# The last chunk of a Fourier-mixing and MLP kernel: sums on VectorE, products read in PSUM, output from three queues

## Chip, cores and metric

One Trainium2 chip, one NeuronCore. The metric is the device time of one execution in microseconds (us). The kernel before takes about 2004 us. Runs with a profile also give the span, from the first to the last recorded instruction, which is 1.8 us less than the time. Two runs of the same kernel can differ by 4 us and more, so this document also uses a measure inside one profile, the **tail**: from the start of the last matmul to the end of the span.

## The reference

```python
def _attn_ref(x):                        # x: 8 x 3008 x 256, float32
    X = np.fft.fft(x, axis=1)
    X = np.fft.fft(X, axis=2)
    return X.real.astype(np.float32)

def _moe_ref(x, w_in, w_out):            # x: 24064 x 256, d_ff 2048
    h = x @ w_in
    relu6 = np.clip(h + 3.0, 0.0, 6.0)
    g = h * relu6 / 6.0
    return (g @ w_out).astype(np.float32)
```

The output of the first goes, reshaped to 24064 x 256, into the second.

## The kernel before

The kernel works through four pairs of batch rows, twelve chunks a pair, eight steps (`fc`) a chunk. In each step TensorE makes the hidden layer (`mlp1`), VectorE and ScalarE gate it, GpSimd forms four sums of the gated blocks (`combine`), and TensorE adds seven products into four PSUM banks (`mlp2`, a seven-multiplication scheme for a 2 x 2 block product). After the last step of a chunk, ScalarE evicts the four banks, GpSimd forms the four output blocks (`finish`), VectorE transposes them in 32 x 32 blocks and SyncE sends them out (`store`). For every chunk but the last of all, `finish` and `store` run beside the next chunk's matmuls. For the last of all, nothing is left to run beside.

```python
    def combine(ch, fc):
        ...
        add(cn[:, 0:2], a[:, 2:3].to_broadcast([P, 2, ch.n]), a[:, 3::-3])
        add(cn[:, 2], cn[:, 0], a[:, 0])
        add(cn[:, 3], a[:, 1], cn[:, 2])
        ch.c[fc] = cn

    def add(out, in0, in1):
        nc.gpsimd.tensor_tensor(out, in0, in1, op=AL.add)

    def mlp2(ch, fc):
        ...
        for i, mv in enumerate(moving):
            ...
            nc.tensor.matmul(ch.acc[i // 2][:, i % 2, 0:ch.n], G[:, i, fc, :], mv, ...)
            if fc == NF - 1 and (i % 2 == 1 or i == 6):
                ...
                k = 2 * (i // 2)
                nc.scalar.mul(ch.e[:, k:i + 1, 0:ch.n], ch.acc[i // 2][:, 0:i + 1 - k, 0:ch.n], 1.0 / WS)

    def finish(ch):
        ...
        add(rn[:, 0, 0], e[:, 0], e[:, 1])
        nc.gpsimd.tensor_tensor(wn[:, 0], e[:, 0], e[:, 5], op=AL.subtract)
        add(wn[:, 1:3], wn[:, 0:1].to_broadcast([P, 2, n]), e[:, 4:2:-1])
        add(rn[:, 0, 1], wn[:, 2], e[:, 6])
        add(rn[:, 1], wn[:, 1:2].to_broadcast([P, 2, n]), e[:, 2:4])

    def store(ch, m):
        ...                              # two transposes, then:
            for qd in range(DB):
                nc.sync.dma_start(out=out_k[...], in_=o[...])
    ...
    # behind the loop over all steps:
    finish(prev)
    for m in range(2):
        store(prev, m)
```

GpSimd also issues all loads of `x` and of the weights: 84 transfers (`nc.gpsimd.dma_start` and the indirect form), the last of them some 630 us before the end.

## Time and profile before

| | before |
|---|---|
| median of 3 runs | 2004.42 us (2000.66 to 2004.54) |
| span of the profiled run | 2002.9 us |
| TensorE busy | 98% |
| start of the last matmul | 1989.4 us |
| end of the last transpose | 1993.95 us |
| start of the last output issue | 2000.0 us |
| end of the span | 2002.9 us (tail 13.5 us) |

The table is to be read from the bottom. TensorE is the bound for 1989 us. Behind its last matmul come 13.5 us in which it has nothing to do: 4.5 us of evictions, sums and transposes, then some 9 us in which only transfers and the closing exchange between engines are left. The change is about these 13.5 us, 0.7% of the time. The views that show this are in the prediction.

### The profile page before, as it was taken

To read this page: it belongs to the slowest core of one execution; us is meant where nothing else is said; L and a number is where in the kernel's file an instruction comes from. 1 tells how busy PE (TensorE), PEld (TensorE's weight loads), DVE (VectorE), ACT (ScalarE), POOL (GpSimd) and SP (SyncE) were. 2 spreads that over 40 slices of the span, in tenths; PEclk is the share of its full clock that TensorE was granted. 3 is DMA by queue.
4 is the path that set the end of the run, shared out by engine and by line. 5 is a ranking of instruction groups with operands and counts; after the bars stand their busy time and mean duration, and the time that the engine had idled before them with its cause. 6 is when DMAs were issued, how large, how long until landed. Compare 5 with 4: busy or idle time off the path is not lost.

```text
span 2002.9 us, 28366 instructions
## 1 busy us (share of the span) xinstructions
PE 1965.6 (98%) x9178; PEld 1691.5 (84%) x9178; DVE 1437.2 (72%) x2701; ACT 701.2 (35%) x1198; POOL 1417.9 (71%) x1612
## 2 busy tenths in 40 slices
PE   9899999999999999999999999999999999999997
PEld 5488888888888888888888888888888888888886
DVE  5677767776777777776777767777678777777775
ACT  6533333333333333333333333333333333333332
POOL 3277778776777787777658877778666667667665
PEclk9899999999999999999999999999999999999998
DMA  9512211211112122110201221112110101101100
GB/s 275 162 27 59 51 40 48 55 38 35 28 35 51 41 51 56 50 51 25 48 18 30 69 56 39 51 43 53 35 27 20 27 17 27 32 12 27 27 11 19
DMA packets 158985, 93.54 MB, mean 47 GB/s; under 512 B 131019, under 2 KB 143819, under 8 KB 158838
## 3 DMA queue, kind: packets, MB, share of 16 engines
q1 hardware_dynamic: 149366, 58.22, 12.1%
q0 software_dynamic: 9472, 33.49, 6.1%
q8 instruction: 75, 1.23, 0.3%
q14 instruction: 72, 0.59, 0.1%
HBM read 54.32 MB, written 37.33 MB: 46 GB/s over the span
## 4 chain that ended last, share of the span: by engine, by line
PE 93%; DVE 3%; ACT 1%; issue 0%; POOL 0%; DVEq 0%; POOLq 0%; ACTq 0%
PE acc L379 55%; PE v L325 16%; PE u L325 16%; PE ps L280 2%; PE ps L226 2%; DVE a L357 1%; ACT t L354 0%; DVE u L338 0%; DVE s L330 0%; ACT PM L457 0%; PE wps L522 0%; DVE o L405 0%; DVE v L344 0%; DVE u L341 0%; PE ps L223 0%
## 5 line engine op out<-in xcount | busy, mean ns | idle before, releaser
L369 POOL TENSOR_TENSOR c<-a 128x512 f32<-128x512 f32 (+1 forms) x384 | 478.4, 1246 | 454.9 <-PE acc L379 358.1
L379 PE MATMUL acc<-c,G 128*128 128x256 f32 (+1 forms) x3072 | 712.1, 375 | 0.0
L354 ACT ACTIVATE t<-u,half 128x512 f32<-128x512 f32 (+2 forms) x416 | 272.4, 655 | 1104.6 <-DVE u L338 1092.9
L379 PEld LDWEIGHTS acc<-c,G 128*128 128x128 f32 x3072 | 577.5, 190 | 72.7
L330 DVE SCALAR_TENSOR_TENSOR s<-qn,WN,u 128x256 f32<-128x256 f32 x768 | 334.6, 477 | 351.6 <-PE u L325 351.2
L379 PE MATMUL acc<-a,G 128*128 128x256 f32 (+1 forms) x2304 | 551.2, 375 | 0.0
L379 PEld LDWEIGHTS acc<-a,G 128*128 128x128 f32 x2304 | 434.6, 190 | 57.6
L325 PE MATMUL v<-q,W 127*128 127x256 f32 x1536 | 397.7, 381 | 7.7 <-DVE a L357 7.7
L325 PE MATMUL u<-q,W 128*128 128x256 f32 x1536 | 395.4, 380 | 2.5 <-DVE a L357 2.2
L325 PEld LDWEIGHTS u<-q,W 128*128 128x128 f32 x1536 | 287.8, 190 | 59.9 <-issue 15.8
L325 PEld LDWEIGHTS v<-q,W 127*128 127x128 f32 x1536 | 289.7, 190 | 55.6 <-issue 8.2
L357 DVE SCALAR_TENSOR_TENSOR a<-t,u 128x512 f32<-128x512 f32 (+2 forms) x416 | 266.1, 646 | 95.7 <-ACT t L354 90.3
L369 POOL TENSOR_TENSOR c<-c,a 128x256 f32<-128x256 f32 (+1 forms) x384 | 274.7, 715 | 30.1
L369 POOL TENSOR_TENSOR c<-a,c 128x256 f32<-128x256 f32 (+1 forms) x384 | 274.6, 715 | 30.1
L338 DVE TENSOR_TENSOR u<-s,v 128x512 f32<-128x512 f32 (+1 forms) x384 | 263.1, 685 | 41.5 <-DVE s L330 0.9
L354 ACT ACTIVATE t<-v,half 128x512 f32<-128x512 f32 (+1 forms) x384 | 257.1, 670 | 5.8 <-DVE v L344 4.5
L344 DVE TENSOR_TENSOR v<-v,s 128x512 f32<-128x512 f32 (+1 forms) x384 | 257.9, 672 | 1.1
L357 DVE SCALAR_TENSOR_TENSOR a<-t,v 128x512 f32<-128x512 f32 (+1 forms) x416 | 255.4, 620 | 0.5
L369 POOL TENSOR_TENSOR r<-w,e 128x256 f32<-128x256 f32 (+1 forms) x96 | 92.2, 981 | 3.8
L385 ACT ACTIVATE e<-acc 128x512 f32<-128x512 f32 (+1 forms) x192 | 87.0, 543 | 2.9 <-PE acc L379 2.8
L405 DVE STREAM_TRANSPOSE o<-r 128x256 f32<-128x256 f32 (+1 forms) x192 | 72.5, 416 | 6.6 <-POOL r L369 6.4
L238 ACT COPY z<-ps 96x512 f32<-96x512 f32 x64 | 37.2, 581 | 83.5 <-PE ps L226 63.1
(81 smaller groups left out, 754.0 us busy)
## 6 DMA issues: line engine op xcount, KB each, us to landing
out_dram<-o SPq DMA_DIRECT2D x736, 32.0 KB
zd<-z SPq DMA_DIRECT2D x32, 384.0 KB
g<-zd SPq DMA_DIRECT2D x48, 256.0 KB
xt<-in_x_dram POOLq DMA_DIRECT2D x21, 384.0 KB, 4.0
qn<-qd SPq DMA_DIRECT2D x23, 256.0 KB
st<-in_moe_w_in_dram POOLq DMA_DIRECT2D x8, 512.0 KB, 11.8
st<-in_moe_w_out_dram POOLq DMA_DIRECT2D x8, 512.0 KB, 5.7
xt<-in_x_dram POOLq DMA_DIRECT2D x7, 376.0 KB, 3.9
```

The lines of the kernel that those rows point to most:

```text
L226: nc.tensor.matmul(ps[0:PZ], F[0:PR, 0:PZ], y[:, 2 * i:2 * i + 2, :], start=True, stop=True)
L280: nc.tensor.matmul(ps[:, blk, 2 * u:2 * u + 2], g[:, kk, blk * (P + 1):blk * (P + 1) + P], T[:, :, gr, blk, kk], start=True, stop=True)
L325: nc.tensor.matmul(ps[:, i], W1[r, blk, f * P:(f + 1) * P], q[r, blk, of:of + KC], start=True, stop=True)
L330: nc.vector.scalar_tensor_tensor(s[:, i].rearrange("p k n -> p (k n)"), qn[:, of * N2:(of + KC) * N2], WN[:, f:f + 1], u[:, i].rearrange(" ...
L338: nc.vector.tensor_tensor(u[:, :, 0:ns], s[:, :, 0:ns], v[:, :, 0:ns], op=AL.add)
L344: nc.vector.tensor_tensor(v[:, :, 0:nm], v[:, :, 0:nm], s[:, :, 0:nm], op=AL.subtract)
L354: nc.scalar.activation(t, h, AF.Relu, bias=half[:], scale=scale)
L357: nc.vector.scalar_tensor_tensor(dst, t, 1.0, h, op0=AL.min, op1=AL.mult)
L369: nc.gpsimd.tensor_tensor(out, in0, in1, op=AL.add)
L379: nc.tensor.matmul(ch.acc[i // 2][:, i % 2, 0:ch.n], G[:, i, fc, :], mv, start=(fc == 0 and i % 2 == 0), stop=(fc == NF - 1), skip_group_c ...
L385: nc.scalar.mul(ch.e[:, k:i + 1, 0:ch.n], ch.acc[i // 2][:, 0:i + 1 - k, 0:ch.n], 1.0 / WS)
L405: nc.vector.transpose(o[:, 0:n // DH, h], ch.r[:, m, h, 0:n].rearrange("p (j i) -> p j i", i=DH))
```

## The change

Its intent is to shorten the tail. (1) The last step's `combine` runs on VectorE, which is free by then. (2) The last chunk's sums run on VectorE, and the products 4, 5 and 6 are read directly in PSUM by a fused multiply-add, so two evictions go. (3) The 16 output transfers are dealt out over SyncE, ScalarE and GpSimd in turn.

```diff
+            self.final = self.last and pr.p == NP - 1
...
+        eng = nc.vector if ch.final and fc == NF - 1 else nc.gpsimd
+        add(cn[:, 0:2], a[:, 2:3].to_broadcast([P, 2, ch.n]), a[:, 3::-3], eng)
+        add(cn[:, 2], cn[:, 0], a[:, 0], eng)
+        add(cn[:, 3], a[:, 1], cn[:, 2], eng)
...
+                if ch.final and k >= 4:
+                    continue
                 nc.scalar.mul(ch.e[:, k:i + 1, 0:ch.n], ...)
...
+    def finish_final(ch):
+        ...
+        def add_product(out, i, in1, sign=1.0):
+            nc.vector.scalar_tensor_tensor(out, ch.acc[i // 2][:, i % 2, 0:n], sign / WS, in1,
+                                           op0=AL.mult, op1=AL.add)
+        add(rn[:, 0, 0], e[:, 0], e[:, 1], nc.vector)
+        turn(ch, os[0], 0, 0)
+        add_product(wn[:, 0], 5, e[:, 0], -1.0)
+        add(wn[:, 2], wn[:, 0], e[:, 3], nc.vector)
+        add_product(rn[:, 0, 1], 6, wn[:, 2])
+        turn(ch, os[0], 0, 1)
+        send(ch, os[0], 0)
+        add_product(wn[:, 1], 4, wn[:, 0])
+        for h in range(2):
+            add(rn[:, 1, h], wn[:, 1], e[:, 2 + h], nc.vector)
+            turn(ch, os[1], 1, h)
+        send(ch, os[1], 1)
...
+        queues = [nc.sync, nc.scalar, nc.gpsimd] if ch.final else [nc.sync]
...
-                nc.sync.dma_start(
+                queues[i % len(queues)].dma_start(
...
-    finish(prev)
-    for m in range(2):
-        store(prev, m)
+    finish_final(prev)
```

`turn` is the transpose of `store`, and `send` its transfers.

More of the change, by code (lines that the diff above doesn't have):

```diff
@@ L362, in combine, with add @@
         cn = c[:, :, 0:ch.n]
-        add(cn[:, 0:2], a[:, 2:3].to_broadcast([P, 2, ch.n]), a[:, 3::-3])
-        add(cn[:, 2], cn[:, 0], a[:, 0])
-        add(cn[:, 3], a[:, 1], cn[:, 2])
+        eng = nc.vector if ch.final and fc == NF - 1 else nc.gpsimd
+        add(cn[:, 0:2], a[:, 2:3].to_broadcast([P, 2, ch.n]), a[:, 3::-3], eng)
+        add(cn[:, 2], cn[:, 0], a[:, 0], eng)
+        add(cn[:, 3], a[:, 1], cn[:, 2], eng)
         ch.c[fc] = cn
-    def add(out, in0, in1):
-        nc.gpsimd.tensor_tensor(out, in0, in1, op=AL.add)
+    def add(out, in0, in1, eng=None):
+        (eng or nc.gpsimd).tensor_tensor(out, in0, in1, op=AL.add)
     def mlp2(ch, fc):
@@ L399, in finish, with turn, send @@
         ch.r = r
+    def finish_final(ch):
+        n = ch.n
+        e = ch.e[:, :, 0:n]
+        w = epool.tile([P, 3, TB], F32, tag="w", bufs=1, name="w")
+        ch.r = epool.tile([P, 2, 2, TB], F32, tag="r", name="r")
+        wn, rn = w[:, :, 0:n], ch.r[:, :, :, 0:n]
+        os = [epool.tile([P, TB // DH, 2, DH], F32, tag="o", name="o") for m in range(2)]
+        def add_product(out, i, in1, sign=1.0):
[13 more added lines that the diff above has]
+        send(ch, os[1], 1)
     def store(ch, m):
-        n = ch.n
         o = epool.tile([P, TB // DH, 2, DH], F32, tag="o", name="o")
         for h in range(2):
-            nc.vector.transpose(o[:, 0:n // DH, h], ch.r[:, m, h, 0:n].rearrange("p (j i) -> p j i", i=DH))
+            turn(ch, o, m, h)
+        send(ch, o, m)
+    def turn(ch, o, m, h):
+        n = ch.n
+        nc.vector.transpose(o[:, 0:n // DH, h], ch.r[:, m, h, 0:n].rearrange("p (j i) -> p j i", i=DH))
+    def send(ch, o, m):
+        queues = [nc.sync, nc.scalar, nc.gpsimd] if ch.final else [nc.sync]
+        i = 0
         sl = 0
@@ L414, in store @@
                 )
+                i += 1
             sl += nb
```

## The prediction

> **What bounds the kernel now.** I read the page first, then the chain of work that ended last from 1970 us on, then the timeline of the last 20 us engine by engine, then the groups with shapes kept apart, and last the rows of the end-of-program line. The page's head says what the kernel is for nearly its whole length:
>
> ```profile
> span 2002.9 us, 28366 instructions
> PE 1965.6 (98%) x9178; PEld 1691.5 (84%) x9178; DVE 1437.2 (72%) x2701; ACT 701.2 (35%) x1198; POOL 1417.9 (71%) x1612
> ```
>
> TensorE is busy 98% of the span, and no engine beside it matters as long as its queue is full. The change leaves all of that alone. The chain, in order of time (start, length, what), shows where TensorE's rule stops:
>
> ```profile
> 1982.90 6.52 PE acc L379 x40
> 1989.42 0.02 issue
> 1989.44 0.50 ACT e L385
> ...
> 1990.01 0.59 POOL w L395
> ...
> 1990.67 0.99 POOL w L369
> ...
> 1992.33 0.96 POOL r L369
> 1993.29 0.02 issue
> 1993.31 0.38 DVE o L405
> ```
>
> The sixth of the seven products leaves TensorE at 1989.42. Then a serial chain runs: ScalarE evicts, GpSimd adds, VectorE transposes. It is 4.5 us long (1989.42 to 1993.95, the end of the second transpose). But the span ends at 2002.9, nearly 9 us later, and the chain as printed says nothing of that stretch. The rows of the output tile and the sync queue's timeline do:
>
> ```profile
> L411 SPq DMA_DIRECT2D out_dram<-o x16: 315/426/499, 1992.8 to 2000.0; - x16
> L405 DVE STREAM_TRANSPOSE o<-r x4: 336/378/379, 1989.4 to 1993.6; 128x192 f32<-128x192 f32 x4
> ```
>
> Sixteen issues from one queue, first start 1992.77, last start 2000.01: 7.24 us over 15 intervals is 0.483 us an issue, 0.43 of it the issue itself. The second half's data were ready at 1993.95, but the queue was still working on the first half's eight issues until 1996.5. So from 1992.77 on the bound is the issuing sequencer. It isn't the transfer: in 1993 to 2003 the DMA view gives the output's packets 17.6% of the 16 engines' time, so 1.76 us if they ran together. After the last issue:
>
> ```profile
> L796 SPq EVENT_SEMAPHORE  x11: 17/28/28, 2000.5 to 2002.8; - x11
> L796 POOLq DRAIN  x3: 51/103/8525, 1991.7 to 2002.6; - x3
> ```
>
> SyncE waits for each landing in turn until 2002.0 (2.0 us after the last issue began), and the closing exchange between the engines takes 0.9 us. From the last issue's start to the end of the span: 2002.9 - 2000.01 = 2.89 us.
>
> **What the Trainium skill says.** (1) "DMA: Bandwidth & Descriptors", section "Issuing engines are not separate DMA queues": starting transfers from several engines saves only the sequencer's time, since all use the same 16 DMA engines. The trace agrees that this is what can be saved here: issue at 0.483 us each, DMA engines under a quarter busy. (2) "Perfetto Trace Analysis", section "DMA Instruction — HWDGE (DVE, Sync)": the descriptor generator is locked for the issuing sequencer's exclusive use, with a lock wait inside the recorded issue. Whether ScalarE's and SyncE's issues therefore exclude each other, no trace of before can show, as only SyncE issues this way; it is my second case below. (3) "VectorE: DVE Perf Modes", section "The TRN2 errata": an fp32 tensor add takes (N+151)/0.96 ns, so 357 ns at 192 columns and 557 ns at 384. The trace is close: 279 ns at 127 columns and 546 ns at 381, against 290 and 554. (4) "DMA: Bandwidth & Descriptors", section "Anatomy of one DMA — SWDGE (gpsimd) path": about 2 us fixed for a transfer, mostly the write's receipt. SyncE's last issue fits (2.0 us). GpSimd's issues here are slower, 3.0 us and more:
>
> ```profile
> L145 POOL DMA_DIRECT2D xt<-in_x_dram x32: 530/552/721, 1.3 to 1369.1; - x32
> ...
> DMA to landing us min/median/max: 3.3/3.9/16.2
> ```
>
> **The change part by part.** The instruction order of the built kernel shows new work only behind the last chunk's last gate; everything ahead of it is the same in order and waits.
>
> *Last combine from GpSimd to VectorE.* It removes three GpSimd adds (996 + 590 + 591 ns, done at 1988.64) and adds three on VectorE (557 + 357 + 357 ns, from about 1986.25 to 1987.7). TensorE had no idle there (its matmuls follow each other to 1989.7, and no wait on GpSimd is listed), so I count 0.
>
> *Final sums on VectorE, three products read from PSUM.* Two of the four evictions (0.50 and 0.32 us) and five GpSimd adds go. Row 341 gives a fused multiply-add touching PSUM 296 ns at 128 columns, and row 330 one 477 ns at 256, so about 0.36 us at 192. The chain now, with about 0.07 us from one VectorE instruction to a dependent one (the gap seen between s and u):
> - r00 = e0+e1 waits for the first eviction (1988.70): 1988.75 to 1989.1; its transpose to 1989.5.
> - w0 from PSUM (its product is there at 1989.42): 1989.55 to 1989.9; w2 to 1990.3; r01 from PSUM to 1990.7; transpose to 1991.1. The first eight transfers can go at 1991.1, against 1992.77: 1.65 us earlier.
> - w1 from PSUM to 1991.45; r10 to 1991.85; transpose to 1992.25; r11 to 1992.6; transpose to 1993.0. The second eight can go at 1993.0, against 1993.95.
>
> *Output from three queues.* Each send gives 3 issues to SyncE, 3 to ScalarE, 2 to GpSimd. SyncE: three issues from 1991.15 are through by 1992.6, before the second send; then 1993.05, 1993.53, 1994.02. With 2.89 us from last issue to end: 1996.9. ScalarE the same, if its issues cost what SyncE's do. GpSimd: two issues of about 0.55 us each (row 145) from 1993.05; the second starts near 1993.7, with a gap as seen between its issues; landing 3.0 us later, 1996.7, plus 0.9: 1997.6. So the software queue ends last, and the span is 1997.6: 5.3 us less. Of this the sums give about 1 us (1993.95 to 1993.0) and the queues the rest.
>
> **The rivals.**
> - *A, as worked out: GpSimd's landing sets the end.* 5.3 us less. For it: the 3.0 us or more of every software issue. Against: those were big loads and these are 16 to 32 KB stores.
> - *B, one descriptor generator for both hardware queues.* Then 12 issues at 0.483 us run one after the other: the first six from 1991.15 to 1994.05, the next six to 1996.95, last start 1996.5, end 1999.4: 3.5 us less. In the profile a ScalarE issue would be longer than 0.43 us while SyncE's runs. For it: the skill's lock. Against: nothing in this trace.
> - *C, GpSimd's stores land as fast as the hardware queue's.* Then the end is 1996.9: 6.0 us less.
> - *D, GpSimd's closing drain takes the place of the wait.* That row shows a drain of 8.5 us, from 1991.7 to 2000.25, 7 us beyond GpSimd's last add (ends 1993.28), and nothing in the profile explains it. It was hidden, as SyncE ended at 2002.0. If it starts anew behind the stores (about 1994.3 + 7 = 2001.3, +0.7) only about 1 us is left. Against: GpSimd's times are rough, and it may just stand for idle time.
> - *E, the last combine slows something.* VectorE is free from 1986.17, so hardly: 0.
> - *F, noise.* The three runs of before lie between 2000.66 and 2004.54, about as far apart as the gain.
>
> **Range and chances.** I weigh A 0.45, B 0.2, C 0.15, D 0.2: 0.45 x 5.3 + 0.2 x 3.5 + 0.15 x 6.0 + 0.2 x 1 = 4.2 us on average, with the middle near 4.8. Two of three runs and the profiled one (2004.63) stand at 2004.5, so I take the median 2004.42 as the base: 2004.4 - 4.8 = 1999.6 us. Range: C together with a run in the faster position of before (-4) gives about 1995; D with no gain beyond 1 us gives 2003.3. I say 1995.0 to 2003.0. Two per cent would be 40 us, more than four times the whole 9 us that follow the last arithmetic; neither side is likely: 0.01 faster, 0.98 within, 0.01 slower.
>
> **What would show each step.** The last transpose ends near 1993.0 instead of 1993.95, and the first output issue starts near 1991.1. TensorE's last matmul still starts at 1989.4 with no new idle. VectorE's fused adds of the last chunk are 0.35 to 0.4 us each. SyncE's last issue starts near 1994.0 (B: 1996.5, and issues on both hardware queues longer than 0.5 us). SyncE's closing waits end near 1996.7 (A) or 1996.0 (C). The prediction is wrong if the closing waits end after 2000 with all issues done by 1995 (D, or an unforeseen landing), or if TensorE shows a wait in the last chunk.

## The result, and the profile after

| | before | after |
|---|---|---|
| median (4 runs each) | 2004.47 us | 2002.32 us |
| range | 2000.66 to 2004.54 | 2000.88 to 2003.66 |
| ratio, 95% interval | | 0.9994, 0.9976 to 1.0011 |
| tail in the profile | 13.5 us | 12.9 us |

A ratio is the mean time of one kernel's runs over that of the other's of the same rounds, so it isn't quite the ratio of the medians. The 4.8 us that I expected are not there: the ratio stands for 1.2 us with an interval that holds zero, and the tail is shorter by 0.6 us.

The head of the page after:

```profile
span 2001.0 us, 28370 instructions
PE 1965.6 (98%) x9178; PEld 1691.6 (85%) x9178; DVE 1440.1 (72%) x2711; ACT 700.3 (35%) x1196; POOL 1416.2 (71%) x1608
```

TensorE's work is the same to 0.1 us. The span is 1.9 us shorter, but 1.3 us of that were there before the change begins: the last chunk's first eviction started at 1988.20 before and at 1986.92 after. The tail compares the rest.

The output's issues, by queue (count, then shortest, median and longest in ns, first and last start); the landing row belongs to GpSimd's issues:

```profile
L451 SPq DMA_DIRECT2D out_dram<-o x6: 316/430/435, 1989.9 to 1992.4; - x6
L451 ACTq DMA_DIRECT2D out_dram<-o x6: 374/438/442, 1989.9 to 1992.5; - x6
L451 POOL DMA_DIRECT2D out_dram<-o x4: 545/565/618, 1990.2 to 1992.4; - x4
...
DMA to landing us min/median/max: 2.0/2.1/2.2
```

All 16 issues have started by 1992.5, in the kernel before by 2000.0. SyncE and ScalarE issue side by side at 0.43 and 0.44 us each. And yet the span ends at 2001.0. The end of the chain that ended last, in order of time (start, length, engine and line):

```profile
1991.19 0.39 DVE o L440
1991.58 0.29 issue
1991.87 0.56 POOL out_dram L451
1992.43 0.53 POOLq L835
```

The chain's last named step is GpSimd's queue at the end-of-program line. That line's own rows in the last 20 us (count, then shortest, median and longest in ns, first and last start):

```profile
L835 SPq EVENT_SEMAPHORE  x12: 17/28/28, 1993.9 to 2001.0; - x12
...
L835 POOLq DRAIN  x3: 46/103/7925, 1992.3 to 2000.7; - x3
L835 SPq DRAIN  x3: 7/7/7, 1995.6 to 2000.5; - x3
```

SyncE's first drain, which follows its wait for the last landing, is at 1995.6: by then every byte is out. Then nothing happens for 4.6 us but one thing: a drain in GpSimd's queue of 7.925 us, from 1992.3 to 2000.2. The closing exchange needs all engines, so it waits for that. The same row before (in the prediction) has 8.525 us from 1991.7, so it ended at 2000.2, and there it was hidden, because SyncE was busy until 2002.0. Hidden by 1.8 us only: whatever one saved at the transfers, no more than that could come out while the drain stayed where it was.

### The profile page after: what moved, and what is told of

Its sections match the earlier page's. It is cut to its first block, busy times and chain, and to the rows that moved or that the text cites. A ratio compares the mean times of both kernels' runs of the same rounds, so it can differ in the third digit from the quotient of the medians.

```text
span 2001.0 us, 28370 instructions
## 1 busy us (share of the span) xinstructions
PE 1965.6 (98%) x9178; PEld 1691.6 (85%) x9178; DVE 1440.1 (72%) x2711; ACT 700.3 (35%) x1196; POOL 1416.2 (71%) x1608
## 4 chain that ended last, share of the span: by engine, by line
PE 93%; DVE 3%; ACT 1%; issue 1%; POOL 0%; DVEq 0%; POOLq 0%; ACTq 0%
PE acc L382 55%; PE v L326 16%; PE u L326 16%; PE ps L280 2%; PE ps L226 2%; DVE a L358 1%; ACT t L355 0%; DVE u L339 0%; DVE s L331 0%; DVE o L440 0%; ACT PM L498 0%; PE wps L563 0%; DVE v L345 0%; DVE u L342 0%; ACT q L282 0%
## 5 line engine op out<-in xcount | busy, mean ns | idle before, releaser
L390 ACT ACTIVATE e<-acc 128x512 f32<-128x512 f32 (+2 forms) x190 | 86.3, 544 | 2.8 <-PE acc L382 2.7
## 6 DMA issues: line engine op xcount, KB each, us to landing
st<-in_moe_w_in_dram POOLq DMA_DIRECT2D x8, 512.0 KB, 11.1
```

## The experiments

**The theory:** GpSimd's closing drain ends some 7 us behind GpSimd's last instruction. The change gave GpSimd four late issues, so the drain stayed late, and it took the place of the wait that was removed. **Rivals:** landings are late when several queues send at once; only GpSimd's own transfers delay the drain; the drain runs to a time of its own.

All tails in one table (end of the span minus start of the last matmul). The drain's end is given behind the end of GpSimd's last instruction, to 0.01 us; it was read from the packed traces, since `prof` prints a drain's start to 0.1 us only. "Hidden" means that SyncE's waits for landings ended later:

| run | tail us | drain's end behind GpSimd's last instruction, us | ratio to before (95%) |
|---|---|---|---|
| before | 13.5 | 6.95 (hidden) | |
| changed | 12.9 | 7.26 | 0.9994 (0.9976 to 1.0011) |
| two_queues | 7.9 | 6.95 (hidden) | 0.998 (0.9967 to 0.9994) |
| gpsimd_sums_two_queues | 11.6 | 6.95 | 0.9993 (0.9978 to 1.0008) |
| late_gpsimd_add | 11.2 | 6.95 | 0.999 (0.9975 to 1.0006) |
| gpsimd_first_half | 11.1 | 7.10 | 0.9988 (0.9973 to 1.0003) |
| after_again (changed) | 12.9 | 7.26 | 0.9992 (0.9975 to 1.0008) |
| two_queues_again | 7.9 | 6.95 (hidden) | 0.998 (0.996 to 1.0001) |
| one_queue | 11.8 | 6.95 (hidden) | 0.9978 (0.9956 to 1.0) |
| gpsimd_combine_two_queues | 8.2 | 6.95 (hidden) | 0.9966 (0.9943 to 0.999) |
| late_gpsimd_memset | 11.0 | 6.95 | one look |
| middle_drain | 7.9 | 2.21 (hidden) | one look |
| drain_after_loads | 8.3 | 1.93 (hidden) | 0.997 (0.9955 to 0.9986) |
| late_add_drain_after_loads | 7.9 | 0.07 (hidden) | one look |
| weights_by_sync | 9.9 | 5.64 | one look |

### two_queues: GpSimd sends nothing

```diff
-        queues = [nc.sync, nc.scalar, nc.gpsimd] if ch.final else [nc.sync]
+        queues = [nc.sync, nc.scalar] if ch.final else [nc.sync]
```

> The changed kernel with its last output sent from SyncE and ScalarE alone (GpSimd issues none). Measured on the tail: from the start of the last matmul to the end of the span (before 13.5 us, changed kernel 12.9 us). Theory, the closing drain: GpSimd's drain ends some 7 us after GpSimd's last instruction, whatever that is; here that is the combine of the last step but one, some 4.9 us ahead of the last matmul, so the drain is over long before SyncE's closing waits. Eight issues a queue: the last starts near 5.1 us after the last matmul's start, plus 2.9: a tail of 8.0 us, and a time 5 to 6 us under the kernel before. Rival, late landings (output written slowly when several queues send at once): the tail stays above 12 us although GpSimd sends nothing. Rival, the drain runs to a time that has nothing to do with GpSimd's work: its end stays 12 us behind the last matmul.

Measured: tail 7.9 us. The median is 1999.86 us against 2003.34 before, and the interval excludes 1. GpSimd's last instruction, from its timeline (start, length):

```profile
1981.38 0.59 POOL L372 TENSOR_TENSOR c<-a,c 128x192 f32<-128x192 f32 x1
```

And the rows of the end-of-program line:

```profile
L835 SPq EVENT_SEMAPHORE  x12: 17/28/28, 1992.3 to 1994.7; - x12
...
L835 POOLq DRAIN  x3: 51/103/7583, 1981.3 to 1994.5; - x3
L835 SPq DRAIN  x3: 7/7/7, 1993.9 to 1994.2; - x3
```

The drain is as long as ever (1981.3 + 7.6 = 1988.9), but it ends 5 us ahead of SyncE's last wait. Late landings are out as a cause. A drain that runs to a time of its own is out too: it moved with GpSimd's last instruction.

### gpsimd_sums_two_queues: the sums back on GpSimd

```diff
-    finish_final(prev)
+    finish(prev)
+    for m in range(2):
+        store(prev, m)
```

(with all four evictions and GpSimd's combine back as well; the output of the last chunk from SyncE and ScalarE)

> The kernel before, all its sums on GpSimd, only its last output sent from SyncE and ScalarE. No GpSimd issue at the end, but GpSimd's last add ends 3.9 us after the last matmul's start. Theory, the drain follows GpSimd's last instruction by 7 us: drain over at 10.9 us, end of the span at 11.5 us (2.0 us less than before). Rival, only GpSimd's own transfers make the drain bind: last issue at 6.7 us, plus 2.9: a tail of 9.5 us (4 us less than before).

Measured: 11.6 us. GpSimd sends nothing here, and the drain, which ends at 1999.3 when SyncE has been done since 1997.4, still sets the end:

```profile
L835 POOLq DRAIN  x3: 51/103/8523, 1990.8 to 1999.8; - x3
L835 SPq DRAIN  x3: 7/7/7, 1997.4 to 1999.5; - x3
```

So a late add holds the drain back as much as a late transfer.

### late_gpsimd_add: one add that nobody needs

```diff
         send(ch, os[1], 1)
+        add(wn[:, 2, 0:64], rn[:, 1, 1, 0:64], rn[:, 1, 0, 0:64])
```

on top of two_queues.

> two_queues plus one GpSimd add of 128x64 elements whose result nobody reads, behind VectorE's last sum. It needs no time of anyone's. Theory, the drain: GpSimd's last instruction then ends 3.4 us after the last matmul's start, the drain at 10.4, the span at 11.1 us: some 3 us longer than two_queues for a 0.3 us instruction. Rival, only transfers from GpSimd count, or late landings: the same tail as two_queues (8.0 us).

Measured: 11.2 us. An add of 0.32 us makes the tail 3.3 us longer. In GpSimd's timeline it is

```profile
1993.95 0.32 POOL L372 TENSOR_TENSOR w<-r 128x64 f32<-128x64 f32 x1 [7.99 <-DVE r L372]
```

and the drains of the end-of-program line are

```profile
L836 POOLq DRAIN  x3: 51/103/7310, 1993.9 to 2001.7; - x3
L836 SPq DRAIN  x3: 7/7/7, 1997.9 to 2001.5; - x3
```

The bracket says that GpSimd had been idle for 8 us before the add. Idleness ahead of the last instruction doesn't help; only quiet behind it does.

### gpsimd_first_half: GpSimd sends in the first half only

```diff
-        queues = [nc.sync, nc.scalar, nc.gpsimd] if ch.final else [nc.sync]
+        queues = ([nc.sync, nc.scalar, nc.gpsimd] if m == 0 else [nc.sync, nc.scalar]) if ch.final else [nc.sync]
```

> The changed kernel, but GpSimd sends only in the first half of the output (2 of 16 transfers, their issues over 3.2 us after the last matmul's start, 1.65 us earlier than the changed kernel's last). Theory, the drain: it ends 1.65 us earlier than in the changed kernel, near 10.5 us, and the tail is 11.2 us. Rival, a drain that runs to a fixed time: 12.9 us as in the changed kernel. Rival, late landings of GpSimd's second half alone: 8 to 9 us.

Measured: 11.1 us. GpSimd's last issue is 1.7 us earlier than in the changed kernel, and the end 1.8 us. The rival with late landings of the second half expected 8 to 9 us and falls.

### after_again and two_queues_again: both on one chip

> The changed kernel again, so that it and two_queues are timed on one chip in the same rounds. The drain theory: tail (last matmul's start to the end of the span) 12.9 us against 13.5 before, so 0.6 us less than before, inside the noise. Rival (the first timing was unlucky): 4 us or more less than before, as the prediction said.

> The version without GpSimd's transfers, beside the changed kernel. The drain theory: tail 7.9 us as in its first run, some 5.6 us under the kernel before and 5.0 under the changed one. Rival: the tail's gain is an accident of one profile, and the times differ from the changed kernel's by no more than 1 us.

Measured: tails 12.9 and 7.9 us as in the first runs. By means of six runs each, the changed kernel took 2003.35 us, two_queues 2000.09 us, the kernel before 2005.12 us (11 runs): two_queues gained 3.3 us on the changed kernel, fewer than the tail's 5.0, and its runs lie between 1995.37 and 2005.39. So the times agree with the tails but don't prove them to the microsecond. Part of the scatter arises in the start-up: in the profiles with weights loaded as before, the first hidden-layer matmul starts between 77.5 and 88.0 us.

### one_queue: the sums alone

```diff
-        queues = [nc.sync, nc.scalar, nc.gpsimd] if ch.final else [nc.sync]
+        queues = [nc.sync]
```

> The change's sums on VectorE alone; the output from SyncE only, as before. First issue 1.8 us after the last matmul's start, the 16th 7.2 us later, plus 2.9: tail 11.9 us, 1.6 us less than before. GpSimd's drain is over 2 us after the last matmul's start and doesn't count. Rival (the changed kernel's loss lies in the sums on VectorE): tail 12.9 us or more.

Measured: 11.8 us. VectorE's sums are worth 1.6 us of tail by themselves. The second queue is worth the other 3.9 (11.8 to 7.9). The timed mean is 4.6 us under before, more than the 1.6 us of the tail; the interval of the ratio reaches 1.0, and I don't read more than the tail out of it.

### gpsimd_combine_two_queues: the combine back on GpSimd

```diff
-        eng = nc.vector if ch.final and fc == NF - 1 else nc.gpsimd
+        eng = nc.gpsimd
```

on top of two_queues.

> two_queues, but the last combine stays on GpSimd as in the kernel before. Its last add ends 0.8 us ahead of the last matmul's start, so the drain ends near 6.2 us, ahead of SyncE's closing waits (7.2). The drain theory: the same tail as two_queues, 7.9 us: the combine's move is worth nothing of its own. Rival (TensorE or VectorE had waited for the combine): 0.5 us more or less.

Measured: 8.2 us. The drain ends at 1996.3 and SyncE's waits at 1997.5, so the drain is hidden here as well, and moving the combine is not needed. Whether it is worth anything stays open: 8.2 lies between the 7.9 of the theory and the 0.5 us more or less of the rival. The 0.3 us more lie behind the last issue, in SyncE's waits for landings; why, no run here tells.

### late_gpsimd_memset: another kind of instruction

```diff
         send(ch, os[1], 1)
+        nc.gpsimd.memset(wn[:, 1, 0:64], 0.0)
```

> two_queues plus one GpSimd memset of 128x64 elements behind VectorE's last sum: an instruction that reads no tensor and moves none by DMA. The drain theory (7 us after GpSimd's last instruction, whatever its kind): the memset ends some 3.4 us after the last matmul's start, the drain near 10.4, the tail is 11.1 us as with the late add. Rival (it needs an add or a transfer; the short drain at the kernel's start, 0.19 us behind four memsets, speaks for it): tail 7.9 us.

Measured: 11.0 us. The kind of the last instruction doesn't matter. But then why was the drain behind the memsets at the kernel's very start 0.19 us long? Something between start and end makes it dear.

### middle_drain: an explicit drain half-way

```diff
+        if p == 1 and ck == 3 and fc == 5:
+            nc.gpsimd.drain()
         if prev and fc < 3:
             finish(prev) if fc == 0 else store(prev, fc - 1)
```

on top of late_gpsimd_add.

> late_gpsimd_add plus one explicit GpSimd drain in the middle of the kernel (second pair, fourth chunk, between two combines). Tells whether the 7 us are paid once (the first drain behind GpSimd work) or by every drain. If by every drain: a drain of some 7 us in the middle, TensorE waits for GpSimd for a few us there, and the closing one still ends 7 us behind the late add (tail 11.1 us). If once: the middle one is long and the closing one is short, tail 7.9 us. If only by the closing one: the middle one is under 1 us and the tail 11.1 us.

Measured: none of the three. The middle drain is long, and the closing one is neither 7 us nor short. GpSimd's timeline around both:

```profile
720.57 0.73 POOL L372 TENSOR_TENSOR c<-a,c 128x256 f32<-128x256 f32 x1
726.29 1.26 POOL L165 TENSOR_TENSOR xt<-xt 94x508 f32<-94x508 f32 x1 [4.98 <-issue]
...
1991.45 0.32 POOL L372 TENSOR_TENSOR w<-r 128x64 f32<-128x64 f32 x1 [7.98 <-DVE r L372]
```

The closing drain's row:

```profile
L838 POOLq DRAIN  x3: 51/103/2562, 1991.4 to 1995.9; - x3
```

GpSimd stood still for 5.0 us at 721.3. The drain's own row (its start is printed to 0.1 us, and it begins beside the add):

```profile
L756 POOLq DRAIN  x1: 5598/5598/5598, 720.5 to 720.5; - x1
```

It ended at 726.1, 4.83 us behind the add (from the packed trace). At the end the drain was over 2.21 us behind the late add, hidden again. TensorE showed no new wait around the middle drain. The 4.8 and 2.2 us add up to 7.0. What a drain costs had been heaped up since the last drain. What had been heaped up isn't time or the number of adds: the middle drain lies a third of the way in. By the counts of transfers in the trace, GpSimd had issued 58 of its 84 transfers before it and 26 behind it. 4.83/58 = 0.083 and 2.21/26 = 0.085 us, and 6.95/84 = 0.083 us in the other kernels. New theory: **a drain takes about 0.083 us for each transfer that GpSimd has issued since its last drain.** With the changed kernel's 88 that gives 7.3 us (7.26 measured twice), with the 86 of gpsimd_first_half 7.1 (7.10).

### drain_after_loads, late_add_drain_after_loads, weights_by_sync: the new theory

The first is the changed kernel, the second late_gpsimd_add, each with a drain behind GpSimd's last load:

```diff
+        if p == NP - 2 and ck == 8 and fc == 5:
+            nc.gpsimd.drain()
```

> The changed kernel as it is, three queues and all, plus one GpSimd drain in the third pair's ninth chunk, behind GpSimd's last load of input and 600 us ahead of the end, where TensorE doesn't wait for GpSimd. New theory: a drain takes about 0.083 us for each transfer that GpSimd has issued since its last drain (84 transfers and 7.0 us in most kernels here, 88 and 7.25 in the changed one, 58 and 5.0 at the middle drain, 26 and 2.2 behind it). Then the early drain takes 7 us beside other work, the closing one has 4 stores to account for, 0.35 us, and SyncE's closing waits set the end again: tail 8.1 us against 12.9 of the changed kernel, some 5 us less than before. Rival (the first drain is dear, a later one takes 2.2 us whatever came between): closing drain 2.2 us, the same tail. Rival (closing drain is dear by itself): tail 12.9 us.

> late_gpsimd_add with the same early drain; no transfer from GpSimd follows it. Theory (cost by transfers since the last drain): the closing drain ends within 0.2 us of the late add, tail 7.9 us. Rival (2.2 us for any later drain): it ends 2.2 us behind the late add; tail 7.9 us also, so the drain's own end tells.

The third is late_gpsimd_add with the 16 weight loads issued by SyncE:

```diff
-            nc.gpsimd.dma_start(out=o, in_=moe_w_in[...])
+            nc.sync.dma_start(out=o, in_=moe_w_in[...])
```

(the same for `moe_w_out`)

> late_gpsimd_add, but the 16 weight loads at the start are issued by SyncE: 68 transfers of GpSimd instead of 84, and about 6400 packets instead of 9472. By transfers: the closing drain ends 5.7 us behind the late add, tail 9.8 us. By packets (0.735 ns each): 4.7 us, tail 8.8 us. Rival (the drain doesn't depend on what was issued): 7.0 us, tail 11.2 us.

With no transfer since the early drain (late_add_drain_after_loads), the closing one is over 0.1 us behind the add. GpSimd's timeline and the drain's row:

```profile
1999.44 0.32 POOL L372 TENSOR_TENSOR w<-r 128x64 f32<-128x64 f32 x1 [7.98 <-DVE r L372]
```

```profile
L838 POOLq DRAIN  x3: 39/103/427, 1999.4 to 2003.9; - x3
```

That rules out "2.2 us for any later drain". The early drain of this kernel, with 84 transfers before it, ended 6.95 us behind the add ahead of it, as the closing drains with 84 do: the cost isn't one of the program's end. With 68 transfers (weights_by_sync) the closing drain ends 5.6 us behind the add (by transfers: 68 x 0.083 = 5.7). The same two views:

```profile
2008.25 0.32 POOL L372 TENSOR_TENSOR w<-r 128x64 f32<-128x64 f32 x1 [7.98 <-DVE r L372]
```

```profile
L836 POOLq DRAIN  x3: 45/103/5997, 2008.2 to 2014.7; - x3
```

My expectation by packets was worked out from too many weight packets: the page has 7168 left, not 6400, so by packets it would be 7168 x 0.735 ns = 5.3 us against 5.64 measured. The kept trace of middle_drain settles the rest: GpSimd's queue moved 6784 packets before the middle drain and 2688 behind it, by packets 5.0 and 2.0 us against 4.83 and 2.21 measured. By bytes it is no better (24.1 MB of 33.5 before the middle drain: 5.0 us; 25.1 MB in weights_by_sync: 5.2 us). A line through the count of transfers, 0.07 us + 0.082 us for each (from 0 and 84), meets all of 26, 58, 68, 86 and 88 within 0.02 us. What the drain does in this time no run tells. (weights_by_sync starts its first chunk 16 to 20 us later than most, so its time is of no use, only its drain.)

drain_after_loads keeps the three queues and has a tail of 8.3 us. Six runs against eleven of the kernel before give a ratio of 0.997 (0.9955 to 0.9986), 6.1 us by the means. The early drain stands beside other work: GpSimd is still from 1402.9 to 1409.96 (the drain ends 6.95 us behind the add, here too), and TensorE's list of waits around it is the same as in two_queues. The closing drain took more than I expected for four transfers. The drains of the end-of-program line:

```profile
L837 POOLq DRAIN  x3: 46/103/2590, 1991.4 to 1995.2; - x3
L837 SPq DRAIN  x3: 7/7/7, 1994.7 to 1995.0; - x3
```

It ends at 1993.9, 1.93 us behind GpSimd's last issue instead of 0.35. These four transfers were still under way, though: the last was issued at 1991.5 and such stores land 2.1 us later, at 1993.6. So here the rule of 0.083 us falls short by 1.6 us. A drain that first waits for every landing and then takes 0.083 us for each is not the answer either: it would end near 1993.9 here, but in the changed kernel, with 88 transfers and the last landing near 1994.5, it would end near 2001.8, and there it ended at 2000.2. A drain that goes through the transfers one by one and is held up only by one that is still under way would suit both; no run tests it, so why the four cost 1.93 us stays open.

## Why the prediction was wrong, point by point

To compare times of the two traces, 1.28 us are added to those of after (first eviction at 1988.20 and 1986.92).

- **TensorE and the combine: right as far as shown.** 0 was counted. TensorE's busy time is unchanged, and gpsimd_combine_two_queues does without the move at a tail 0.3 us longer, for a reason that no run tells.
- **VectorE's chain: right.** First send predicted at 1991.1, measured 1991.2; second 1993.0, measured 1992.9. Fused adds 0.32 to 0.36 us against 0.36.
- **SyncE's issues: right.** Last issue predicted 1994.02, measured 1993.7. ScalarE's issues cost what SyncE's do, so rival B (one generator that they lock in turn) was wrong.
- **A's landing: two thirds of its size.** 3.0 us from big loads had been taken for small stores; they land in 2.1 us, as C had it. The prediction's fourth citation is about GpSimd's path, so SyncE's 2.0 us was no test of its 2 us; these stores are.
- **SyncE's closing waits: right by luck.** "near 1996.7 (A)" against 1996.9. But GpSimd's last landing, which was to end them at 1996.7, came near 1995.9 (1994.65 in the packed trace, plus 1.28). SyncE then spent another 0.95 us on the waits that remained, which A had not counted: two errors cancel.
- **The share of the sums: too small.** "Of this the sums give about 1 us (1993.95 to 1993.0)" compares when the second half is ready. With one queue, which the prediction itself calls the bound from its first issue on, what counts is when the first half can go: 1.65 us earlier by its own figures, and one_queue measured 1.6.
- **The failing step is "So the software queue ends last, and the span is 1997.6", with D at 0.2.** Not GpSimd's landing but GpSimd's drain ended last. D had the size ("about 1994.3 + 7 = 2001.3, +0.7 only about 1 us is left"; measured 0.6 us of tail; the drain's end predicted at 2001.3, measured at 2000.2 + 1.28 = 2001.5) and the reason, and I discounted it with "it may just stand for idle time". The test that I skipped costs nothing: 8.5 us in a closing row, ending (at 2000.2; the prediction's 2000.25 is a slip) 1.8 us ahead of the wait that I was about to shorten by 5 us. Even as mere idle time it had to be given a cause before it could be passed over.
- **The middle and the range.** The range held the median of 2002.32, but not for its reason: the gain that it was built around, 4.8 us, was measured as 1.2 us in the ratio and 0.6 us in the tail. Nor does "the middle near 4.8" follow from the chances: their mean is 4.2 and their median is A's 5.3. And the end that the prediction gives D with its 1 us, 2003.3 (2004.4 - 1 is 2003.4), lies above the top of the range, 2003.0, although D had a chance of 0.2.
- **What the change lost and where.** Sums on VectorE 1.6 us (one_queue) and a second hardware queue 3.9 us (two_queues): 5.6 us of tail (13.5 to 7.9) were there to be had. The third queue, GpSimd's, took 5.0 of them back.

## What to carry to other kernels

Before you shorten the wait that sets the end, list every other engine's closing rows and see by how much each is hidden: the smallest such margin caps the gain. If GpSimd issues transfers, keep it quiet for its last drain's length (here 7 us for 84 transfers) or give it an explicit drain early, where its time is free. A queue added to the end of a kernel is worth the issuing time that it saves less what its engine then still has to do: here ScalarE's queue beside SyncE's gave 3.9 us, and GpSimd's took 5.0.

## What the Trainium skill lacked or had wrong

- "VectorE: DVE Perf Modes", section "The DRAIN you can't avoid", tells of closing drains of about 12 ns on all five engines. GpSimd's ended 6.95 to 7.26 us behind its last instruction in most kernels here, about 0.083 us for each transfer that GpSimd had issued since its last drain (0 transfers: 0.07 us; 26: 2.21; 58: 4.83; 68: 5.64; 84: 6.95; 86: 7.10; 88: 7.26). No page has this dependence.
- "Perfetto Trace Analysis", section "DMA Instruction — HWDGE (DVE, Sync)", has the descriptor generator locked for one sequencer at a time. SyncE and ScalarE issued side by side here, both starting at 1989.9, at medians of 0.430 and 0.438 us in the changed kernel, with none longer than 0.442, where SyncE alone took 0.426 in the kernel before. No lock wait between these two shows; a lock held for a small part of an issue isn't ruled out.
